# The second network product in float16 pairs, scaled by powers of two

## The chip, the core and the metric

The kernel runs on one core of one Trainium2 chip. The metric is the device time of a launch in microseconds, the median of several runs. The engines are TensorE (PE, its weight loads shown as PEld), VectorE (DVE), ScalarE (ACT), GpSimd (POOL), and SyncE (SP), which issues most DMAs. PSUM holds the products of TensorE until another engine moves them out.

## The reference

An attention block with heads mixed before and after the softmax, then a gated network (SwiGLU) behind an RMS norm. B, H, S, D = 4, 12, 448, 64; DM = 768, DFF = 1536; all inputs float32.

```
scores = q @ k^T / sqrt(D);  scores = einsum('bhij,hg->bgij', scores, w_pre)
attn   = softmax(scores);    attn   = einsum('bhij,hg->bgij', attn, w_post)
x      = (attn @ v) as 1792 tokens x 768
xn     = x / sqrt(mean(x^2) + 1e-6) * rms_g
h      = silu(xn @ w_gate) * (xn @ w_val)        1792 x 1536
out    = h @ w_out                               1792 x 768
```

## The kernel before

Part A (`part_a`, up to about 345 us of the trace) is the attention; it leaves x in DRAM. Part B (`part_b`) is the network, and the change lies there.

A product that must be more exact than one pass of TensorE's narrow types is made of pairs: an operand is split into hi, its value rounded to the narrow type, and lo, the remainder. `product` (L653) does three matmuls for each of six blocks of 128 rows: hi by hi, hi by lo, lo by hi, so 18 matmuls of 128x128 by 128x448 into one PSUM tile. The narrow type is fp32r (float32 storage, "f32" in the rows of matmuls) in some places and float16 in others.

**First product.** The loop over f (12 blocks of 128 columns of the gate and value weights, in the order of `ROWS`, so that blocks of the first and the second half of h take turns) and b (4 batches of 448 tokens) does two `product`s, pg and pv. Rows f = 0 to 3 (f < `PLAIN`) use fp32r pairs, rows 4 to 11 float16 pairs of x (`xn`) and of the weights. The weights come as 64-bit floats; a conversion (`load_w`: `begin`, an Abs on ACT that waits for the DMA of `wraw`, then `half`, four DVE instructions L517 to L520) makes float32 of them. `convert(f)` starts one conversion, if one is due, and gives back its second step. For a float16 row `half` also sums magnitudes (L559), and `even(f + 1, p)` turns the sums into a scale that is a power of two: `largest` (L572 to L578) finds the greatest over all partitions with short DVE instructions, `power` (L585 to L589) makes the power of two and its inverse and copies them to all partitions; then come hi on ACT (L874) and lo on DVE (L875). It was called for p = 0 at b = 2 and p = 1 at b = 3, ahead of `convert`. The outputs' weights (`queue_out`, kind "out") are converted to float32 in rows 5 to 10, at b = 2 and 3, and kept whole in `wos`.

`swiglu` (L683) evicts pg and pv into h: in float16 rows a Silu on ACT and one DVE instruction (L696). h then feeds Strassen's scheme (7 products in place of 8): sums and differences of the blocks of h (first or second half of its 1536 rows, even or odd batch) are made on POOL (L702) and stored to DRAM as `td[0]` to `td[6]`, for two pairs of batches g.

**Second product.** The loop over n (the 7 Strassen products), g (2 pairs of batches) and j (3 blocks of output rows) is 42 units. `hs[n, g]`, one operand, is loaded (`h_load`, `hraw`) and split by `h_split`, two splits per unit: hi on ACT (L643), lo on DVE (L644). The splits run one n ahead of TensorE: twelve are made in f = 11 (b = 2 and 3), so hs[1, 0] is made in the units 0 to 2 of n = 0 and hs[1, 1] in the units 3 to 5. Three buffers (`h_tile`) take turns. The other operand, `fac[n, j]`, is made by `factor`: hi on ACT (L829), lo on POOL (L830); `before` combines weight blocks on POOL (`mix`, L834) ahead of it. A unit's `po` is moved out by ACT for n = 0 (L1025), later by DVE with an addition (L1027).

Every engine works its instructions off in the order of the program, which is written out by hand (`manual_schedule`); a DVE instruction that stands behind a late one is late as well. `ps_p` has 6 PSUM buffers, and one unit of the first product uses two of them.

Of the kernel before, what the change touches and what calls it, by code (L numbers as in the profile page):

```python
# [23 lines left out]
SP_ = 460  # L24
# [24 lines left out]
def attention_moe(ctx: ExitStack, tc, q, k, v, wpre, wpost, mask, ident, wgv, wo, rms_g, out):  # L49
# [473 lines left out]
    def load_w(src, kind, pool_name=None, plain=None):  # L523

        wr, wp_ = b_pools["wr"], b_pools.get(pool_name)
        raws, pair, words = {}, [], {}

        def fetch(p, eng):
            ks = slice(KT * p, KT * p + KT)
            raws[p] = wr.tile([128, KT * 128, 2], I32, name="wraw", tag="wraw", bufs=2)  # L530
            eng.dma_start(raws[p].rearrange("p n t -> p (n t)"), src[:, ks].rearrange("p a f -> p (a f)").bitcast(I32))

        def begin(p):
            raw = raws[p]
            if kind != "out" and not p:
                pair.extend(wp_.tile([128, FT, 128], F32R, name=f"w{n}", tag=f"w{n}") for n in "hl")
            if plain is None:
                c = wr.tile([128, KT * 128], I32, name="wc", tag="wc", bufs=2)
            else:
                c = half.place(2 * half.at + p)  # L540
                plain.append(c)
            words[p] = c
            nc.scalar.activation(c.bitcast(F32), raw.bitcast(F32)[:, :, 1], AF.Abs)

        def half(p):
            raw, c = raws[p], words[p]
            for op in to_f32(raw, c, c)[1:]:
                op()
            if kind == "wide":
                ks = slice(KT * p, KT * p + KT)  # L550
                hi, lo = pair
                f = c.bitcast(F32).rearrange("p (a f) -> p a f", f=128)
                nc.scalar.activation(hi[:, ks], f, AF.Copy)
                nc.gpsimd.tensor_tensor(lo[:, ks], f, hi[:, ks].bitcast(F32), ALU.subtract)
            elif kind == "narrow":
                half.plain.append(c.bitcast(F32))
                if not p:
                    half.sums = b_pools["tiny"].tile([128, 8], F32, name="wsum", tag="wsum", bufs=2)
                nc.scalar.activation(narrow(pair)[0][:, KT * p : KT * p + KT], half.plain[p].rearrange("p (a f) -> p a f", f=128), AF.Abs, scale=2.0 ** -12, accum_out=half.sums[:, p : p + 1])  # L559

        half.fetch, half.begin, half.pair, half.plain = fetch, begin, pair, []
        return half

# [14 lines left out]
        nc.vector.transpose(z[:, 0], z[:, 1])  # L578
        return z[:, 0, :1]

    def power(t, up, more, name):
        o = b_pools["tiny"].tile([128, 3], F32, name=name, tag=name, bufs=2)
# [17 lines left out]
        return t[:, :KT], t[:, KT:]  # L600

    def h_tile(i):
        if i == 0:
            t = b_pools["narrow"].tile([128, 2 * KT, S], F32R, name="hn", tag="xn01")
        else:
            t = b_pools["x3" if i == 1 else "x"].tile([128, 2 * KT, S], F32R, name=f"h{i}", tag="x3" if i == 1 else "x0")
        return t[:, :KT], t[:, KT:]

    raws = {}

# [26 lines left out]
    def h_split(n):  # L637
        for _ in range(min(n, len(hr))):
            i, g, kk, raw = hr.pop(0)
            if kk == 0:  # L640
                hs[i, g] = h_tile((2 * i + g) % 3)
            hi, lo = (t[:, kk] for t in hs[i, g])
            nc.scalar.activation(hi, raw, AF.Copy)  # L643
            nc.vector.tensor_tensor(lo, raw, hi.bitcast(F32), ALU.subtract)  # L644

    def both(ps, w, x, kk):
        (wh, wl), (xh, xl_) = w, x
# [11 lines left out]
            nc.tensor.matmul(ps, a2, xh[:, kk], start=False, stop=(kk == KT - 1))  # L659

    w, xs, wos, fac, hs, hr, keep, unit, xn = {}, {}, {}, {}, {}, [], {}, {}, {}

    conv = {}

# [18 lines left out]
    def swiglu(b, f, pg, pv):  # L683
        half, kk = divmod(ROWS[f], KT)
        i, odd = divmod(b, 2)
        sg = t_tile("sg")
        h = keep["11", i] if not (half or odd) else sg
        if f < PLAIN:
            g, u = (t_tile(n) for n in "gu")
            nc.vector.tensor_tensor(g, pg, ry[b], ALU.mult)  # L690
            nc.scalar.activation(sg, g, AF.Silu)
            nc.vector.tensor_tensor(u, pv, ry[b], ALU.mult)
            nc.gpsimd.tensor_tensor(h, sg, u, ALU.mult)
        else:
            nc.scalar.activation(sg, pg, AF.Silu, scale=unit[f])
            nc.vector.scalar_tensor_tensor(h, pv, unit[f], sg, ALU.mult, ALU.mult)  # L696

        def out_(n, t):
# [93 lines left out]
    def part_b(ps_p):  # L792
# [26 lines left out]
        def factor(n, j):  # L819
            src = block(*((0, 0), (0, 1), (0, 0), (0, 0), (1, 1), (1, 0), (0, 1))[n], j)  # L820
            side = "b" if n % 2 else "a"
            if j == 2 and n % 2 == 0:
                t = b_pools["wr"].tile([128, FT, 128], F32R, name="fac", tag="wraw", bufs=2)
            else:
                pl, tag = (b_pools["keep"], "e1") if j == 2 else (b_pools["w2" + side], ("wh", "wl")[j])
                t = pl.tile([128, FT, 128], F32R, name="fac", tag=tag)
            hi, lo = t[:, :KT], t[:, KT:]
            f = src.rearrange("p (a f) -> p a f", f=128)
            nc.scalar.activation(hi, f, AF.Copy)  # L829
            nc.gpsimd.tensor_tensor(lo, f, hi.bitcast(F32), ALU.subtract)  # L830
            fac[n, j] = hi, lo

        def mix(o, x, y, op=ALU.subtract):
# [29 lines left out]
                nc.vector.tensor_scalar(held["g"], g_sb, up, None, ALU.mult)  # L863
            return held

        def even(f, p, held={}):
            half = halves[f]
            if not p:
                held["up"], unit[f] = power(largest(half.sums, 2), 2, gain(2)["down"], "unit")
                w[f] = narrow(half.pair)  # L870
            up = held["up"]
            hi, lo = (t[:, KT * p : KT * p + KT] for t in w[f])
            c = half.plain[p].rearrange("p (a f) -> p a f", f=128)
            nc.scalar.activation(hi, c, AF.Copy, scale=up)  # L874
            nc.vector.scalar_tensor_tensor(lo, c, up, hi, ALU.mult, ALU.subtract)  # L875

        ahead_x = [(b, kk) for b in range(B) for kk in range(KT)]
        loaded, ry_ps = [], [None]
# [32 lines left out]
        def first_row():  # L911
# [29 lines left out]
            swiglu(2, 0, *first_ps[2])  # L941
            last_rms(0)
            x_fetch(3)

        def last_rms(stage):
            if stage == 0:
# [15 lines left out]
        for f in range(1, FT):  # L962
            plain = f < PLAIN
            for b in range(B):
# [8 lines left out]
                even_next = PLAIN - 1 <= f < FT - 1  # L973
                product(pg, (hi[:, :KT], lo[:, :KT]), x)
                product(pv, (hi[:, KT:], lo[:, KT:]), x)
                if even_next and b >= 2:
                    even(f + 1, b - 2)
                second = convert(f)
                rest = x_narrow(AT_ONCE[f][b]) if plain else None
                second()  # L980
                if plain:
                    rest()
                swiglu(b, f, pg, pv)
                if f == 1 and b == 0:
                    last_rms(1)
# [23 lines left out]
        for n in range(7):  # L1009
            for j, g in units:  # L1010
                po = ps_p.tile([128, S], F32, name="po", tag="p")
                product(po, fac[n, j], hs[n, g])
                h_split(2)
                h_load(4)
                store()
                o = None
# [4 lines left out]
                    stores.append((out[e * 128 : e * 128 + 128, b * S : b * S + S], o))  # L1021
                u_, t_ = u[j, g], t[j, g]
                adds = [[], [(o, u_)], [(u_, u_)], [(t_, u_)], [(o, t_)], [(o, t_), (u_, u_)], [(o, u_)]]
                if not n:
                    nc.scalar.activation(u_, po, AF.Copy)  # L1025
                for dst, add in adds[n]:
                    nc.vector.tensor_tensor(dst, po, add, ALU.add)  # L1027
                if not g:
                    before(n, j)
        store()  # L1030
# [88 lines left out]
```

## Time and profile before

| | us |
|---|---|
| median of 3 runs | 854.97 (850.5 to 855.56) |
| profiled execution | 852.61 |
| its span, first to last instruction | 850.7 |
| PE busy | 815.2 (96%) |
| DVE busy | 613.7 (72%) |
| ACT busy | 420.4 (49%) |
| POOL busy | 360.7 (42%) |

Part A ends and part B begins near 345 us. The fp32r rows of the first product take the time up to 473.9 us, its float16 rows 473.9 to 693.0, the second product 693.0 to 846.9. A row of the timeline gives the start in us, the duration in us, engine, line of the kernel, operation, what it writes and reads, shapes, and in brackets the idle time before it and what ended it. Ends of matmuls are modelled, so the distance between two starts is what is read of them.

### The profile page before, as it was taken

To read this page: it belongs to the slowest core of one execution; us is meant where nothing else is said; L and a number is where in the kernel's file an instruction comes from. 1 tells how busy PE (TensorE), PEld (TensorE's weight loads), DVE (VectorE), ACT (ScalarE), POOL (GpSimd) and SP (SyncE) were. 2 spreads that over 40 slices of the span, in tenths; PEclk is the share of its full clock that TensorE was granted. 3 is DMA by queue.
4 is the path that set the end of the run, shared out by engine and by line. 5 is a ranking of instruction groups with operands and counts; after the bars stand their busy time and mean duration, and the time that the engine had idled before them with its cause. 6 is when DMAs were issued, how large, how long until landed. Compare 5 with 4: busy or idle time off the path is not lost.

```text
span 850.7 us, 26665 instructions
## 1 busy us (share of the span) xinstructions
PE 815.2 (96%) x10900; PEld 608.1 (71%) x10900; DVE 613.7 (72%) x1119; ACT 420.4 (49%) x931; POOL 360.7 (42%) x497
## 2 busy tenths in 40 slices
PE   6899998999999899899999999999999999999998
PEld 2557686777777787689999555555555569999997
DVE  5777686788777676779678867777877459976561
ACT  3677675777767676653334243423333246353310
POOL 8233444555545347944663511212112168572210
PEclk9999998999999999999999999999999999999999
DMA  7687567866855654663655354665647257564641
GB/s 215 200 231 229 165 216 209 238 183 192 246 184 179 197 172 130 187 219 118 196 161 166 108 156 150 198 191 158 194 115 251 76 162 216 161 186 130 173 131 65
DMA packets 81021, 150.07 MB, mean 176 GB/s; under 512 B 10767, under 2 KB 70317, under 8 KB 80899
## 3 DMA queue, kind: packets, MB, share of 16 engines
q1 hardware_dynamic: 76286, 134.72, 52.1%
q0 software_dynamic: 3648, 11.31, 4.9%
q10 hardware_dynamic: 965, 2.34, 0.8%
q8 instruction: 86, 1.41, 0.7%
q14 instruction: 36, 0.29, 0.1%
HBM read 77.55 MB, written 31.21 MB: 128 GB/s over the span
## 4 chain that ended last, share of the span: by engine, by line
PE 75%; DVE 9%; DMA 7%; issue 4%; ACT 2%; POOL 2%; SPq 0%; DVEq 0%; POOLq 0%; ACTq 0%
PE pm L226 9%; PE sp L185 8%; PE qk L137 8%; PE av L270 7%; PE po L659 6%; PE po L657 6%; PE po L658 6%; PE pv L659 4%; PE pv L658 4%; PE pv L657 4%; PE pg L658 4%; PE pg L659 4%; PE pg L657 4%; DMA r<-st 3%; DMA xs<-xd 2%
## 5 line engine op out<-in xcount | busy, mean ns | idle before, releaser
L185 PE MATMUL sp<-r,wk_pre 64*64 64x448 f32 x720 | 165.9, 547 | 5.4 <-DMA r<-st 1.6
L137 PE MATMUL qk<-k,q 64*64 64x448 f32 x768 | 156.8, 564 | 5.9 <-DMA q<-in_q 4.3
L199 ACT ACTIVATE e<-sp,nm 128x448 f32<-128x448 f32 x180 | 114.5, 639 | 90.6 <-DVE nm L192 88.9
L192 DVE TENSOR_REDUCE nm<-sp 128x1 f32<-128x448 f32 x180 | 111.6, 623 | 60.5 <-PE qk L137 32.1
L226 PEld LDWEIGHTS pm<-wn,e 60*64 60x64 f32 x5152 | 110.6, 135 | 48.0 <-POOL wn L211 21.3
L211 POOL TENSOR_SCALAR wn<-wk,rp 128x60 f32<-128x60 f32 x180 | 55.8, 322 | 163.1 <-DVE rp L208 138.7
L226 PE MATMUL pm<-wn,e 60*64 60x60 f32 x5152 | 109.1, 221 | 14.3 <-issue 11.2
L702 POOL TENSOR_TENSOR keep<-sg,keep 128x448 f32<-128x448 f32 x24 | 28.8, 1202 | 164.0 <-DVE sg L696 119.7
L270 PE MATMUL av<-at_all,v 64*64 64x240 f32 (+4 forms) x1728 | 94.9, 321 | 3.3 <-issue 3.3
L185 PEld LDWEIGHTS sp<-r,wk_pre 64*64 64x64 f32 x720 | 62.3, 134 | 24.2 <-issue 10.8
L270 PEld LDWEIGHTS av<-at_all,v 64*64 64x64 f32 x1728 | 71.1, 134 | 6.3 <-issue 5.9
L137 PEld LDWEIGHTS qk<-k,q 64*64 64x64 f32 x768 | 55.1, 136 | 26.5 <-issue 7.3
L659 PE MATMUL pv<-xn,wl 128*128 128x448 f16 x192 | 67.7, 352 | 0.6 <-DVE wl L875 0.6
L657 PE MATMUL pv<-xn,wh 128*128 128x448 f16 x192 | 67.7, 352 | 0.3 <-ACT wh L874 0.3
L657 PE MATMUL pg<-xn,wh 128*128 128x448 f16 x192 | 67.7, 353 | 0.0
L658 PE MATMUL pv<-xn,wh 128*128 128x448 f16 x192 | 67.7, 352 | 0.0
L658 PE MATMUL pg<-xn,wh 128*128 128x448 f16 x192 | 67.7, 352 | 0.0
L659 PE MATMUL pg<-xn,wl 128*128 128x448 f16 x192 | 67.7, 352 | 0.0
L239 DVE COPY at_all<-pm 128x420 f32<-128x420 f32 x92 | 54.3, 591 | 16.8 <-PE pm L226 16.4
L830 POOL TENSOR_TENSOR fac<-wo,fac 128x768 fp32r<-128x768 f32 x21 | 42.2, 2027 | 51.6 <-ACT fac L829 51.6
L659 PEld LDWEIGHTS <-wl 128*128 128x128 f16 x384 | 37.6, 98 | 36.1 <-DVE wl L875 1.1
L657 PEld LDWEIGHTS <-wh 128*128 128x128 f16 x384 | 37.6, 98 | 35.7 <-ACT wh L874 0.7
(169 smaller groups left out, 1883.5 us busy)
## 6 DMA issues: line engine op xcount, KB each, us to landing
r<-st SPq DMA_DIRECT2D x117, 210.0 KB
hraw<-td SPq DMA_DIRECT2D x84, 224.0 KB
wraw<-in_wgv SPq DMA_DIRECT2D x20, 768.0 KB
td<-keep SPq DMA_DIRECT2D x48, 224.0 KB
wraw<-in_wo SPq DMA_DIRECT2D x12, 768.0 KB
r<-st SPq DMA_DIRECT2D x44, 175.0 KB
v<-in_v SPq DMA_DIRECT2D x24, 256.0 KB
q<-in_q POOLq DMA_DIRECT2D x28, 192.0 KB, 5.4
```

The costliest lines, as they stand in the source:

```text
L137: nc.tensor.matmul(ps[j][m, :S], qt[n][sl, hp, m], kt[n // NC, hp][sl], start=True, stop=True)
L185: nc.tensor.matmul(o, wk_pre[sl], rt[n][sl, 2 * p + v_], start=True, stop=True)
L192: nc.vector.tensor_reduce(t, ps[:, :S], AX.X, ALU.max, negate=True)
L199: nc.scalar.activation(e, ps[:, :S], AF.Exp, bias=nmx.pop((n, p, u)), accum_out=sm[n, p][:, u : u + 1])
L211: nc.gpsimd.tensor_scalar(wn[n, p][:, u], wk, r[:, u : u + 1], 1.0, ALU.mult, ALU.mult)
L226: nc.tensor.matmul(o[:, :, at_], e[u_][sl, j : j + JT], w_, start=True, stop=True)
L239: nc.vector.tensor_copy(dst, src)
L270: nc.tensor.matmul(x, vt[b, hp][sl, j, c_], a, start=(c_ == 0), stop=(c_ == JC - 1))
L657: nc.tensor.matmul(ps, a, xh[:, kk], start=(kk == 0), stop=False)
L658: nc.tensor.matmul(ps, a, xl_[:, kk], start=False, stop=False)
L659: nc.tensor.matmul(ps, a2, xh[:, kk], start=False, stop=(kk == KT - 1))
L830: nc.gpsimd.tensor_tensor(lo, f, hi.bitcast(F32), ALU.subtract)
```

## The change

h and the outputs' weights become float16 pairs (hi and lo are both float16) in place of fp32r pairs. Float16 has a narrow range, so both are first multiplied by powers of two, which come from sums of magnitudes; the inverses are multiplied in when `po` is evicted from PSUM.

- `magnitude`: an Abs on ACT with the sum of each partition as a second result, for each of the 12 "out" halves (in `half`) and, through `count`, for each of the 48 tiles of h, one unit after `swiglu` made it.
- `scale_out(j, stage)`: `largest` and `power` for a block j of outputs' weights, and its four pieces multiplied in place on ACT; in rows f = 7 and 9 over b = 0 to 3, and for j = 2 in f = 11 at b = 0 and 1.
- `scale_of(n, cols)`: a DVE reduce (or three) over columns of sums, `largest`, `power`, and one multiplication for the inverses. `scale_of(0)`, for td[0], in f = 11 at b = 0; `scale_of(1)`, for g = 0 of the others, in f = 11 at b = 3, ahead of that unit's `swiglu`; `scale_of(2)`, for g = 1 of the others, in n = 0, unit j = 1 of g = 0, after that unit's two splits.
- `h_split`: hi is a copy with a scale; lo is one DVE instruction that multiplies, then subtracts hi.
- The evictions multiply by the inverse, `down`.
- `even` no longer takes p: at b = 2 it does the scale and both hi parts at once, behind `convert`'s first step, and both lo parts after `convert`'s second step.

```diff
+            else:
+                at_ = 48 + 2 * (half.at % 2) + p
+                magnitude(c.bitcast(F32), KT * 128, small[0][:, at_ : at_ + 1])
...
-            nc.scalar.activation(hi, raw, AF.Copy)
-            nc.vector.tensor_tensor(lo, raw, hi.bitcast(F32), ALU.subtract)
+            sc = scale_h[1 + g if i else 0]
+            nc.scalar.activation(hi, raw, AF.Copy, scale=sc)
+            nc.vector.scalar_tensor_tensor(lo, raw, sc, hi, ALU.mult, ALU.subtract)
...
+    def magnitude(x, n, out_):
+        nc.scalar.activation(small[1].bitcast(F16)[:, :n], x, AF.Abs, scale=2.0 ** -12, accum_out=out_)
+
+    def count():
+        for b, f, h in marks:
+            (g, odd), (half, kk) = divmod(b, 2), divmod(ROWS[f], KT)
+            at_ = ((2 * g + half) * 2 + odd) * KT + kk
+            magnitude(h, S, small[0][:, at_ : at_ + 1])
+        marks.clear()
...
+        def even(f):
...
+            for c, hi, lo in parts:
+                nc.scalar.activation(hi, c, AF.Copy, scale=up)
+
+            def rest():
+                for c, hi, lo in parts:
+                    nc.vector.scalar_tensor_tensor(lo, c, up, hi, ALU.mult, ALU.subtract)
+
+            return rest
+
+        def scale_out(j, stage):
+            if stage == 0:
+                o = small[0][:, 64 + 3 * j : 67 + 3 * j]
+                power(largest(small[0][:, 48:64], 4), 0, None, None, o)
+            for c in wos[2 * j + stage // 2][stage % 2 :][:1]:
+                c = c.bitcast(F32)
+                nc.scalar.activation(c, c, AF.Copy, scale=small[0][:, 65 + 3 * j : 66 + 3 * j])
+
+        def scale_of(n, cols):
+            t = small[0][:, 100 : 104]
+            for i, x in enumerate(cols):
+                nc.vector.tensor_reduce(t[:, i : i + 1], x, AX.X, ALU.max)
+            if len(cols) > 1:
+                nc.vector.tensor_reduce(t[:, :1], t[:, : len(cols)], AX.X, ALU.max)
+            o = small[0][:, 80 + 3 * n : 83 + 3 * n]
+            scale_h[n], down = power(largest(t, 1), 0, None, None, o)
+            downs = small[0][:, 64:73].rearrange("p (j c) -> p j c", c=3)[:, :, 2]
+            nc.vector.tensor_scalar(small[0][:, 90 + 3 * n : 93 + 3 * n], downs, down, None, ALU.mult)
...
-                if even_next and b >= 2:
-                    even(f + 1, b - 2)
-                second = convert(f)
-                rest = x_narrow(AT_ONCE[f][b]) if plain else None
-                second()
+                todo_ = [convert(f)]
+                if even_next and b == 2:
+                    todo_.append(even(f + 1))
                 if plain:
-                    rest()
+                    todo_.append(x_narrow(AT_ONCE[f][b]))
+                count()
+                for x in todo_:
+                    x()
+                if f in (FT // 2 + 1, FT // 2 + 3):
+                    scale_out((f - FT // 2) // 2, b)
+                if f == FT - 1:
+                    if b == 0:
+                        scale_out(2, 0)
+                        scale_of(0, [small[0][:, :KT], small[0][:, 24 : 24 + KT]])
+                    if b == 1:
+                        for i in range(1, 4):
+                            scale_out(2, i)
+                    if b == 3:
+                        scale_of(1, [small[0][:, :24]])
                 swiglu(b, f, pg, pv)
...
                 product(po, fac[n, j], hs[n, g])
+                if n == j == g == 0:
+                    count()
                 h_split(2)
+                if not n and not g and j == 1:
+                    scale_of(2, [small[0][:, 24:48]])
...
-                    nc.scalar.activation(u_, po, AF.Copy)
+                    nc.scalar.activation(u_, po, AF.Copy, scale=down)
                 for dst, add in adds[n]:
-                    nc.vector.tensor_tensor(dst, po, add, ALU.add)
+                    nc.vector.scalar_tensor_tensor(dst, po, down, add, ALU.mult, ALU.add)
```

The tiles of h (`h_tile`) and of the weights (`factor`) keep their sizes in bytes and their places.

## Rows read from the trace of the kernel before

**Rows 1.** Busy us of each engine by stretch: PE, PEld, DVE, ACT, POOL, PEclk, DMA.

```profile
480.00:640.00 160.00, 160.00 (x847) 82.76 (x846) 120.93 (x200) 54.31 (x85) 31.22 (x26) 1.00 0.54 159
692.00:720.00 28.00, 28.00 (x141) 25.63 (x139) 26.02 (x17) 14.59 (x28) 23.68 (x12) 1.00 0.74 230
720.00:760.00 40.00, 40.00 (x198) 36.85 (x198) 32.79 (x35) 17.62 (x31) 25.13 (x12) 1.00 0.59 174
```

**Rows 2.** Tile po: durations in ns (min/median/max), first and last start in us.

```profile
L659 PE MATMUL po<-h,fac x162: 360/363/369, 704.4 to 846.5; 128*128 128x448 f32 x162
...
L657 PE MATMUL po<-hn,fac x90: 360/366/529, 693.0 to 835.2; 128*128 128x448 f32 x90
```

**Rows 3.** Tile xn, the same view.

```profile
L657 PE MATMUL pg<-xn,wh x192: 352/352/363, 473.9 to 689.2; 128*128 128x448 f16 x192
...
L659 PE MATMUL pv<-xn,wl x192: 352/352/363, 479.0 to 693.0; 128*128 128x448 f16 x192
```

**Rows 4.** Timeline of PE, 475.5 to 480.5 us: start, duration, line, operation, idle before.

```profile
477.17 0.35 PE L659 MATMUL pg<-xn,wl 128*128 128x448 f16 x1
477.82 0.36 PE L657 MATMUL pv<-xn,wh 128*128 128x448 f16 x1 [0.30 <-ACT wh L874]
...
479.02 0.36 PE L659 MATMUL pv<-xn,wl 128*128 128x448 f16 x1 [0.65 <-DVE wl L875]
```

**Rows 5.** Timeline of DVE, 466 to 480 us: ends of a chain of twelve.

```profile
467.33 0.17 DVE L572 COPY wsum<-wsum 64x2 f32<-64x2 f32 x1
...
470.18 0.16 DVE L589 COPY unit<-unit 64x2 f32<-64x2 f32 x1
```

**Rows 6.** Timeline of DVE, 570 to 585 us, row f = 7.

```profile
571.77 1.05 DVE L573 COPY wsum<-wsum 32x4 f32<-32x4 f32 x1
...
575.16 0.16 DVE L589 COPY unit<-unit 64x2 f32<-64x2 f32 x1
...
577.32 0.55 DVE L517 TENSOR_SCALAR wo<-wo 128x768 f32<-128x768 f32 x1
...
579.50 0.96 DVE L520 SCALAR_TENSOR_TENSOR wo<-wraw,wo 128x768 int32<-128x768 int32 x1
```

**Rows 7.** Timeline of POOL, the same stretch.

```profile
571.68 1.13 POOL L702 TENSOR_TENSOR keep<-sg,keep 128x448 f32<-128x448 f32 x1 [11.84 <-DVE sg L696]
```

**Rows 8.** Timeline of DVE, 686 to 694 and 709 to 716 us.

```profile
691.20 0.62 DVE L644 TENSOR_TENSOR hn<-hraw,hn 128x448 fp32r<-128x448 f32 x1 [0.93 <-ACT hn L643]
693.43 0.68 DVE L696 SCALAR_TENSOR_TENSOR sg<-pv,unit,sg 128x448 f32<-128x448 f32 x1 [1.60 <-PE pv L659]
...
708.36 6.66 DVE L644 TENSOR_TENSOR h<-hraw,h 128x448 fp32r<-128x448 f32 x3
```

**Rows 9.** Timeline of POOL, 692 to 722 us, and line 830's durations (ns).

```profile
712.29 4.43 POOL L834 TENSOR_TENSOR wo<-wo 128x768 f32<-128x768 f32 x2
716.68 2.24 POOL L830 TENSOR_TENSOR fac<-wo,fac 128x768 fp32r<-128x768 f32 x1
...
L830 POOL TENSOR_TENSOR fac<-wo,fac x21: 1819/1919/2285, 671.0 to 808.7; 128x768 fp32r<-128x768 f32 x21
```

**Rows 10.** Timeline of ACT, 557 to 587 us.

```profile
562.93 0.84 ACT L559 ACTIVATE wh<-wc 128x768 f16<-128x768 f32 x1 [3.69 <-DVE wc L520]
563.68 0.19 ACT L559 ACTIVATION_READ_ACCUMULATOR wh<-wc 128x1 f32 x1
```

**Rows 11.** Lines 627 and 875: durations in ns, min/median/max.

```profile
L627 DVE SCALAR_TENSOR_TENSOR x<-raw,g_sb,x x6: 673/676/1822, 374.4 to 378.5; 128x448 fp32r<-128x448 f32 x6
...
L875 DVE SCALAR_TENSOR_TENSOR wl<-wc,unit,wh x16: 1006/1018/1890, 471.4 to 662.9; 128x768 f16<-128x768 f32 x16
```

**Rows 12.** Timeline of SP's DMA issues and of ACT, 557 to 592 us.

```profile
562.90 0.33 SPq L531 DMA_DIRECT2D wraw<-in_wo  x1
...
580.53 0.33 SPq L531 DMA_DIRECT2D wraw<-in_wgv  x1
...
585.72 0.92 ACT L543 ACTIVATE wc<-wraw 128x768 f32<-128x768 f32 x1 [4.08 <-DMA wraw<-in_wgv]
```

More of the change, by code (lines that the diff above doesn't have):

```diff
@@ L579, in largest, with power @@
         return z[:, 0, :1]
-    def power(t, up, more, name):
-        o = b_pools["tiny"].tile([128, 3], F32, name=name, tag=name, bufs=2)
+    def power(t, up, more, name, o=None):
+        if o is None:
+            o = b_pools["tiny"].tile([128, 3], F32, name=name, tag=name, bufs=2)
         p, s_, inv = (o[:, i : i + 1] for i in range(3))
@@ L602, in h_tile @@
     def h_tile(i):
[L603 to L607, printed above, removed]
+        pl, tag = (("narrow", "xn01"), ("x3", "x3"), ("x", "x0"))[i]
+        t = b_pools[pl].tile([128, 4 * KT, S], F16, name=f"h{i}", tag=tag)
+        return t[:, :KT], t[:, KT : 2 * KT]
     raws = {}
@@ L661, in attention_moe @@
     w, xs, wos, fac, hs, hr, keep, unit, xn = {}, {}, {}, {}, {}, [], {}, {}, {}
+    scale_h, marks, small = {}, [], []
+    def magnitude(x, n, out_):
[6 more added lines that the diff above has]
+        marks.clear()
     conv = {}
@@ L696, in swiglu @@
             nc.vector.scalar_tensor_tensor(h, pv, unit[f], sg, ALU.mult, ALU.mult)
+        marks.append((b, f, h))
         def out_(n, t):
@@ L822, in factor @@
             if j == 2 and n % 2 == 0:
-                t = b_pools["wr"].tile([128, FT, 128], F32R, name="fac", tag="wraw", bufs=2)
+                t = b_pools["wr"].tile([128, 2 * FT, 128], F16, name="fac", tag="wraw", bufs=2)
             else:
                 pl, tag = (b_pools["keep"], "e1") if j == 2 else (b_pools["w2" + side], ("wh", "wl")[j])
-                t = pl.tile([128, FT, 128], F32R, name="fac", tag=tag)
-            hi, lo = t[:, :KT], t[:, KT:]
+                t = pl.tile([128, 2 * FT, 128], F16, name="fac", tag=tag)
+            hi, lo = t[:, :KT], t[:, KT:FT]
             f = src.rearrange("p (a f) -> p a f", f=128)
             nc.scalar.activation(hi, f, AF.Copy)
-            nc.gpsimd.tensor_tensor(lo, f, hi.bitcast(F32), ALU.subtract)
+            nc.gpsimd.tensor_tensor(lo, f, hi, ALU.subtract)
             fac[n, j] = hi, lo
@@ L864, in gain @@
             return held
-        def even(f, p, held={}):
+        def even(f):
             half = halves[f]
[L868 to L875, printed above, removed]
+            up, unit[f] = power(largest(half.sums, 2), 2, gain(2)["down"], "unit")
+            w[f] = narrow(half.pair)
+            parts = [(c.rearrange("p (a f) -> p a f", f=128), *(t[:, KT * p : KT * p + KT] for t in w[f])) for p, c in enumerate(half.plain)]
+            for c, hi, lo in parts:
[21 more added lines that the diff above has]
+            nc.vector.tensor_scalar(small[0][:, 90 + 3 * n : 93 + 3 * n], downs, down, None, ALU.mult)
         ahead_x = [(b, kk) for b in range(B) for kk in range(KT)]
@@ L943, in first_row @@
             x_fetch(3)
+            small.extend(const.tile([128, SP_], F32, name=n, tag="sum", bufs=2) for n in ("small", "junk"))
         def last_rms(stage):
@@ L1023, in part_b @@
                 adds = [[], [(o, u_)], [(u_, u_)], [(t_, u_)], [(o, t_)], [(o, t_), (u_, u_)], [(o, u_)]]
+                k_ = 90 + 3 * (1 + g if n else 0) + j
+                down = small[0][:, k_ : k_ + 1]
                 if not n:
-                    nc.scalar.activation(u_, po, AF.Copy)
+                    nc.scalar.activation(u_, po, AF.Copy, scale=down)
                 for dst, add in adds[n]:
-                    nc.vector.tensor_tensor(dst, po, add, ALU.add)
+                    nc.vector.scalar_tensor_tensor(dst, po, down, add, ALU.mult, ALU.add)
                 if not g:
```

## The prediction

> **What bounds the kernel now.** The busy times by stretch come first [rows 1]. In the stretches that the change touches TensorE is busy from end to end, at the full granted clock (1.00, the 2.4 GHz level): the reader is to see 28.00 of 28 us and 40.00 of 40. So what counts is the step from one matmul's start to the next one's, and the places where TensorE stood waiting. The second network product (tile po: 42 units, each 18 matmuls and an eviction, 756 matmuls in all) starts at 693.0 and its last matmul at 846.5 [rows 2]: 153.5 / 755 = 203.3 ns a step. The gate and value products of float16 pairs (tile xn, 1152 matmuls of the same 128x128 by 128x448) start at 473.9, the last one at 693.0 [rows 3]: 219.1 us over 1151 steps. Three of these, from 477.17 to 479.02, hold two waits [rows 4]: 1.85 us where three steps are 0.57, so 1.28 too long; (219.1 - 1.28) / 1151 = 189.2 ns. The type makes 14.1 ns a matmul. The profiled run took 852.61 us, of which the span is 850.7.
>
> Next, the vector engine (DVE) and GpSimd (POOL) at the start of the second product: busy 26.02 and 23.68 of 28 us [rows 1]. A split on DVE (L644, two inputs in SBUF) takes 0.62 alone, at 691.20, but three take 6.66 at 708.36 [rows 8], 2.2 each, as long as the POOL instructions beside them [rows 9]: DVE gets one such instruction done for each of POOL's, until POOL pauses at 716.68 + 2.24 = 718.9. The short instructions that find a scale show the same in an earlier row of units: L573, a copy of four numbers, took 1.05 and ended at 571.77 + 1.05 = 572.82 [rows 6], POOL's L702 at 571.68 + 1.13 = 572.81 [rows 7].
>
> **The matmuls, a gain of 10.6 us.** h and the outputs' weights become float16 pairs of the shapes of [rows 3], so the step is taken as 189.2: 755 x 14.1 ns = 10.6. Bounds: nothing (third rival), and 10.7, by the rows' rounding.
>
> **The weights of the next row, a gain of 1.3 us.** even() now does both parts at b = 2; before, the second came at b = 3, and the two waits of [rows 4] were for its wh and wl. At b = 2 of that row the chain L572 to L589 ends at 470.34 [rows 5]. Two copies on ACT and two subtractions of 1.0 us alone [rows 11], 1.9 beside POOL, follow with some 1.3 us of other work: done by 475.5, ahead of the 477.82 at which they are wanted. So 1.3, with 0 as the other end.
>
> In rows f = 5 to 10 these subtractions now stand behind the four conversion instructions, and the copies behind the Abs that waits for wraw. Take f = 7. The chain ends at 575.3 [rows 6], conversion (L517 to L520) takes 580.46 - 577.32 = 3.1, two subtractions 2.0: 580.4. Row f = 8 starts at 473.9 + 1.3 + 4 x 144 x 0.1892 = 584.2. The wraw in question was issued at 562.90; one issued at 580.53 let its reader start at 585.72 [rows 12], 5.2 later, so it lands near 568, before ACT gets to the Abs. Cost nothing; the cover is 3.8 us a row, and past it each us is paid once a row.
>
> **Magnitudes and scalings on ACT, cost nothing.** 48 Abs over h and 12 over weights, each with a read of its sum, cost at most the 0.84 + 0.19 of the 768-column one [rows 10]; with 12 scalings of 768 columns at about 1 us, 74 us of ACT in the 455 from the first. ACT was busy 14.59 of 28 us at most [rows 1]; an h is read a unit after it is made, and nothing on TensorE waits for a magnitude alone. Evictions become three-operand instructions, 0.68 as the swiglu's at 693.43 where a two-operand one takes 0.62 [rows 8]; six PSUM buffers cover them, but for the last: 0.06 us.
>
> **The third scale, a cost of 4.7 us.** scale_of is a reduce, the twelve instructions L572 to L589 and a multiplication, about 3.4 us (3.0 by [rows 5], and 0.4). scale_out and scale_of(0) fall where DVE may trail by a unit. scale_of(1), at f = 11 and b = 3, stands behind the split that ends at 691.82 and ahead of the swiglu at 693.43 [rows 8]: that swiglu starts near 695.2, and POOL's burst, which begins with its result, shifts by 1.8. scale_of(2), in unit j = 1 of n = 0, stands between splits 4 and 5 of hs[1, 0]. Split 4 ended at 708.36 + 2.2 = 710.6, now at 712.4. POOL instructions, which ended at 712.3, 714.5, 716.7 and 718.9 [rows 9], now do so at 714.1, 716.3, 718.5 and 720.7. Four of the chain's instructions move two or more numbers of a row (L573, L577, L588, L589); by [rows 6, 7] each waits for one of these ends. So the scale is there at 720.7, and splits 5 and 6 at 721.6 and 722.3. TensorE wants split 5's low half as matmul 121 after the first: 693.0 + 121 x 0.1892 = 715.9 (before, 717.6). It waits 5.7. With less of DVE against it POOL is faster (L830: 1.82 to 2.29 [rows 9]), which may give 1 back: 4.7. The ends: if the chain runs free, it is through at 715.8, and split 5 waits for the POOL end at 716.3 or 718.5, split 6 for the next, so about 2; if POOL gains nothing, 6. I take 4.7, since the row nearest to it (L573) shows the lock in full. Behind it, hs[1, 1] is wanted from 728 on, and POOL pauses, because its next factors wait for ACT's copies, which stand behind the same scale. Later on POOL is busy 25.13 of 40 us, against 23.68 of 28 [rows 1].
>
> **Sum.** -10.6 - 1.3 + 4.7 + 0.1 = -7.1: 852.61 becomes 845.5. The profiled run lies 2.4 under the median of the three (854.97); the mean of all four is 853.4, which becomes 846.3. I say 846.
>
> A rule of the Trainium skill speaks against the new split, which multiplies and subtracts in one three-operand instruction: "Vector Engine (DVE) Microarchitecture Reference", section 7, "Points that are easy to get wrong", says that this form, with two SBUF inputs that aren't bf16, runs at half the throughput. The rows disagree with it (fourth rival). By the page the sum would be about 2 us worse.
>
> **Rivals.** First, no wait at the third scale: POOL's burst thins out, or the chain is through before it matters. For it: each L830 stands behind a copy on ACT, which leaves holes. Against it: [rows 8, 9]. A gain of 11.8, so 841.5. Chance 0.17.
>
> Second, more waits than that one. hs[0, 1] keeps about 1 us of cover after the shift by 1.8, and in rows f = 1 to 3 DVE runs behind TensorE (the wait of [rows 4] is its doing) and now has magnitudes between its conversions, on ACT. Two or three waits of 1 to 3 us leave a gain of 0 to 4: 849 to 853. Chance 0.18.
>
> Third, the step isn't the type's, and the change doesn't do what it says. For it: the two products ran beside different traffic, a DMA share of 0.54 against 0.74 and 0.59 [rows 1]. Against it: the float16 steps stayed at 189 whatever ran beside them. Then -1.3 + 4.7 + 0.1 leaves 856 to 857. Chance 0.04.
>
> Fourth, splits at half rate. The three-operand form took 1.02 us for 768 columns and 0.68 for 448 [rows 11], 1.06 ns a column, so one a cycle of DVE's; doubled, a split takes 1.15. Splits 5 and 6 of hs[1, 0] come 0.9 later and the next six use up their cover: 848. Chance 0.03.
>
> Fifth, on the other side, slower: in rows f = 4 to 10 the subtractions behind the conversion come late for the next row. Slower by over 1% needs 8.5 + 7.1 = 15.6 us lost, over seven rows 2.2 each, so a lateness of 3.8 + 2.2 = 6.0 in every row, for instance by wraw landing at 577 or the new Abs holding up ACT's copies: from 862 on. Against it: DVE is busy 120.93 of 160 us there [rows 1], 20.6 of the 27.2 of a row, and only rows 7 and 9 get a chain more. Chance 0.06.
>
> **How the numbers follow.** My forecast, a wait of 2 to 6 us at the third scale alone, has 0.52: 843.5 to 848, likeliest 846. Over 1%, 8.5 us, is about what a measurement of this kernel can tell from no change. A third of the forecast's cases (0.17), with a wait under 3.3 us, and the first rival (0.17) pass it: faster 0.34. Slower 0.06; the rest, 0.60, is within 1%. The range from 840.5 to 852.5 takes in the first rival and most of the second, with the scatter of 2.5 us that the runs show; it leaves out the slower cases and about one in ten below it and above.
>
> **What would show it.** Right: a step of po of 189 ns; no wait ahead of row f = 4; one wait of 3 to 6 us in the seventh unit of po, put down to DVE's h, and in the chain ahead of it L573, L577, L588 and L589 at 1 to 2 us each. Wrong: that chain free of POOL, waits in units 3 to 5 of po or late ones, or waits for wl at the start of rows 5 to 11.

## The result, and the profile after

The change brought no gain. The comparison gave 854.54 us against 848.86 for the kernel before, medians of 20 runs each, and a ratio of 1.0051 (95% interval 1.0031 to 1.0072). This ratio and those below are worked out from the fast runs (one of the changed kernel, 861.93 us, was slow), so they are not quite the quotients of the medians. On two more chips the ratio was 0.9997 (0.9967 to 1.0027) and 0.9992 (0.9962 to 1.0022), and the kernel before against itself gave 0.9965 (0.9935 to 0.9996), so a few tenths of a per cent are not to be read from one comparison. What is to be explained is that a gain of about 12 us, all of it there, was given back: 846 was forecast, and 850.9 to 854.5 came.

The profiled execution of the changed kernel took 851.36 us, its span 849.4. The attention, which the change leaves alone, differs by 3.2 us between the two profiled executions, so part B is compared by itself, from the first matmul of the first product to the last matmul: 346.0 to 846.5 before, 342.8 to 845.2 after, 500.5 and 502.4 us. Later executions gave 501.4 for the kernel before, 501.7 and 501.1 for the changed one. All these lengths are differences of starts read to 0.1 us.

From the page of the changed kernel: busy time of PE, the chain that ended last by engine, and two groups of matmuls (busy us and mean ns, idle time before them and its releaser).

```profile
PE 804.5 (95%) x10900; PEld 538.4 (63%) x10900; DVE 633.1 (75%) x1199; ACT 477.2 (56%) x1063; POOL 355.6 (42%) x497
...
PE 47%; DVE 27%; issue 8%; ACT 8%; DMA 7%; POOL 2%; SPq 1%; ACTq 0%; DVEq 0%; POOLq 0%
...
L662 PE MATMUL po<-h,fac 128*128 128x448 f16 x252 | 89.9, 357 | 6.2 <-DVE h L648 6.2
...
L663 PE MATMUL pg<-xn,wl 128*128 128x448 f16 x192 | 67.7, 353 | 4.3 <-DVE wl L893 4.3
```

Most of the loss is in the two idle times: TensorE waits 6.2 us for low halves of h, and 4.3 us for low halves of gate and value weights. Its busy time by stretch (columns as in [rows 1]) shows where:

```profile
480.00:640.00 160.00, 157.63 (x833) 81.23 (x832) 122.42 (x215) 79.23 (x152) 29.68 (x24) 1.00 0.53 155
692.00:720.00 28.00, 24.74 (x130) 12.57 (x129) 26.29 (x42) 14.23 (x25) 21.16 (x12) 1.00 0.68 214
...
720.00:760.00 40.00, 37.10 (x184) 18.65 (x184) 33.04 (x38) 20.80 (x34) 23.55 (x14) 0.91 0.63 191
```

In [rows 1] PE was busy for the whole of all three. The timeline of PE has four long waits (start, duration, idle before the matmul in brackets):

```profile
637.25 0.36 PE L663 MATMUL pg<-xn,wl 128*128 128x448 f16 x1 [2.16 <-DVE wl L893]
...
666.60 0.36 PE L663 MATMUL pg<-xn,wl 128*128 128x448 f16 x1 [1.93 <-DVE wl L893]
...
708.35 0.35 PE L662 MATMUL po<-h,fac 128*128 128x448 f16 x1 [1.42 <-DVE h L648]
...
722.90 0.53 PE L662 MATMUL po<-h,fac 128*128 128x448 f16 x1 [4.75 <-DVE h L648]
```

Counted as the step from one matmul's start to the next, less the 0.19 of a free one, that is 2.3 us at the start of row f = 10, 2.1 at f = 11 (and 0.4 at f = 9), 1.6 in the fourth unit of the second product ("unit 3"), and 4.9 in the seventh ("unit 6"). During the last one the granted clock fell to 0.50, the 1.2 GHz level, and stayed there for 4.8 us behind it:

```profile
721.00:727.50 6.50, 4.60 (x13) 1.92 (x13) 6.07 (x10) 5.47 (x10) 0.98 (x1) 0.50 0.54 160
```

Thirteen matmuls came 0.37 us apart there in place of 0.19, 2.3 us more. The losses in order: 4.8 + 1.6 + 4.9 + 2.3 = 13.6 us. On the other side stand the 10.6 and 1.3 us of the prediction's first two terms. -11.9 + 13.6 = +1.7, against a measured 502.4 - 500.5 = +1.9.

### The profile page after: what moved, and what is told of

It is laid out like the page before. It is cut to its first block, busy times and chain, and to the rows that moved or that the text cites. A ratio compares the mean times of both kernels' runs of the same rounds, so it can differ in the third digit from the quotient of the medians.

```text
span 849.4 us, 26853 instructions
## 1 busy us (share of the span) xinstructions
PE 804.5 (95%) x10900; PEld 538.4 (63%) x10900; DVE 633.1 (75%) x1199; ACT 477.2 (56%) x1063; POOL 355.6 (42%) x497
## 4 chain that ended last, share of the span: by engine, by line
PE 47%; DVE 27%; issue 8%; ACT 8%; DMA 7%; POOL 2%; SPq 1%; ACTq 0%; DVEq 0%; POOLq 0%
PE pm L226 9%; PE qk L137 8%; PE sp L185 8%; PE av L270 7%; PE po L662 5%; PE po L663 5%; PE po L661 5%; DVE wc L519 3%; DVE wc L518 3%; DMA xs<-xd 2%; DMA r<-st 2%; DVE wc L520 2%; DVE wc L517 2%; ACT wc L543 2%; DVE wo L519 1%
## 5 line engine op out<-in xcount | busy, mean ns | idle before, releaser
L185 PE MATMUL sp<-r,wk_pre 64*64 64x448 f32 x720 | 163.7, 539 | 4.2 <-DMA r<-st 2.5
L137 PE MATMUL qk<-k,q 64*64 64x448 f32 x768 | 152.3, 554 | 6.0 <-DMA q<-in_q 4.1
L662 PE MATMUL po<-h,fac 128*128 128x448 f16 x252 | 89.9, 357 | 6.2 <-DVE h L648 6.2
L661 PE MATMUL po<-h,fac 128*128 128x448 f16 x252 | 89.7, 356 | 0.0
L663 PE MATMUL po<-h,fac 128*128 128x448 f16 x252 | 89.7, 356 | 0.0
L648 DVE SCALAR_TENSOR_TENSOR h<-hraw,small,h 128x448 f16<-128x448 f32 x84 | 82.7, 1027 | 7.8 <-ACT h L647 7.7
L647 ACT ACTIVATE h<-hraw,small 128x448 f16<-128x448 f32 x84 | 51.6, 659 | 49.3 <-PE po L663 28.6
L661 PE MATMUL pg<-xn,wh 128*128 128x448 f16 x192 | 67.7, 352 | 0.0
```

Of the source, the lines that this page charges most:

```text
L137: nc.tensor.matmul(ps[j][m, :S], qt[n][sl, hp, m], kt[n // NC, hp][sl], start=True, stop=True)
L185: nc.tensor.matmul(o, wk_pre[sl], rt[n][sl, 2 * p + v_], start=True, stop=True)
L647: nc.scalar.activation(hi, raw, AF.Copy, scale=sc)
L648: nc.vector.scalar_tensor_tensor(lo, raw, sc, hi, ALU.mult, ALU.subtract)
L661: nc.tensor.matmul(ps, a, xh[:, kk], start=(kk == 0), stop=False)
L662: nc.tensor.matmul(ps, a, xl_[:, kk], start=False, stop=False)
```

## The loop that falls behind

The waits at rows 9 to 11 were not in the sum, so their cause was looked for first. DVE's swiglu instruction of a row's last block (b = 3), in rows f = 6 to 10 of the changed kernel:

```profile
554.89 0.68 DVE L711 SCALAR_TENSOR_TENSOR sg<-pv,unit,sg 128x448 f32<-128x448 f32 x1 [1.58 <-ACT sg L710]
...
586.11 0.68 DVE L711 SCALAR_TENSOR_TENSOR sg<-pv,unit,sg 128x448 f32<-128x448 f32 x1 [2.41 <-ACT sg L710]
...
613.81 0.68 DVE L711 SCALAR_TENSOR_TENSOR sg<-pv,unit,sg 128x448 f32<-128x448 f32 x1 [1.58 <-ACT sg L710]
...
645.02 0.68 DVE L711 SCALAR_TENSOR_TENSOR sg<-pv,unit,sg 128x448 f32<-128x448 f32 x1 [2.41 <-ACT sg L710]
...
672.72 0.69 DVE L711 SCALAR_TENSOR_TENSOR sg<-pv,unit,sg 128x448 f32<-128x448 f32 x1 [1.58 <-ACT sg L710]
```

Rows 7 to 10 take 31.2, 27.7, 31.2 and 27.7 us, where TensorE needs 144 x 0.1892 = 27.2. In each of these five lines, DVE's idle time ends with ACT's Silu, not with TensorE's product: DVE and ACT pace each other. The end of row 8 shows how. ACT, then DVE, same stretch:

```profile
612.32 0.84 ACT L669 ACTIVATE junk<-wo 128x768 f16<-128x768 f32 x1 [2.47 <-DVE wo L520]
613.07 0.19 ACT L669 ACTIVATION_READ_ACCUMULATOR junk<-wo 128x1 f32 x1
613.16 0.61 ACT L710 ACTIVATE sg<-pg,unit 128x448 f32<-128x448 f32 x1
613.68 0.89 ACT L543 ACTIVATE wc<-wraw 128x768 f32<-128x768 f32 x1
```

```profile
611.27 0.96 DVE L520 SCALAR_TENSOR_TENSOR wo<-wraw,wo 128x768 int32<-128x768 int32 x1
613.81 0.68 DVE L711 SCALAR_TENSOR_TENSOR sg<-pv,unit,sg 128x448 f32<-128x448 f32 x1 [1.58 <-ACT sg L710]
614.61 0.56 DVE L517 TENSOR_SCALAR wc<-wc 128x768 f32<-128x768 f32 x1
```

The magnitude of the outputs' weights (junk<-wo) cannot begin before DVE has made the last quarter of the conversion (L520, done at 612.23). The Silu stands behind it on ACT, the swiglu (L711) waits for the Silu, and the next conversion (L517) stands behind the swiglu, and its Abs on ACT (L543) behind the Silu. DVE idles 1.58 us, though TensorE was through with row 8 at 606.9. In rows 7 and 9 `scale_out` adds a chain on DVE and a scaling on ACT, again ahead of the Silu. So a row with conversions has no time to spare, and whatever a row is late stays for the next one. The subtractions that make wl for the next row drift with the loop (DVE, in rows 6 and 8, both subtractions in one line):

```profile
547.70 1.94 DVE L893 SCALAR_TENSOR_TENSOR wl<-wc,unit,wh 128x768 f16<-128x768 f32 x2
...
606.61 1.94 DVE L893 SCALAR_TENSOR_TENSOR wl<-wc,unit,wh 128x768 f16<-128x768 f32 x2
```

They lie 58.9 us apart, 29.5 a row against TensorE's 27.2. The first of the two was done 4.1 us before row 7's third matmul wanted it, 1.8 us before row 8's, and after that each row's third matmul waited: 0.4, 2.3 and 2.1 us.

## The experiments

Two theories stood at the start, for two different losses. The loop just shown, for rows 9 to 11; and, for units 3 and 6, the chains of `scale_of` in DVE's queue, stretched by POOL. The rival was that the losses come from something the scales only accompany (the float16 pairs themselves, the new order of `even`, other traffic). The first four kernels ran on one chip, where the kernel before took 853.7 us (845.83 to 859.04).

**Magnitudes and scaling out of the loop.** The weights' magnitudes wait for the next `count()`, which takes h's; `scale_out` goes behind `swiglu`.

```diff
-                magnitude(c.bitcast(F32), KT * 128, small[0][:, at_ : at_ + 1])
+                out_marks.append((c.bitcast(F32), at_))
...
         marks.clear()
+        for c, at_ in out_marks:
+            magnitude(c, KT * 128, small[0][:, at_ : at_ + 1])
+        out_marks.clear()
...
-                if f in (FT // 2 + 1, FT // 2 + 3):
-                    scale_out((f - FT // 2) // 2, b)
                 swiglu(b, f, pg, pv)
+                if f in (FT // 2 + 1, FT // 2 + 3):
+                    scale_out((f - FT // 2) // 2, b)
```

> The changed kernel with one order altered: the magnitudes of the outputs' weights wait for the next unit's count, and scale_out stands behind swiglu, so ACT reaches Silu without first waiting for DVE's conversion. Theory 'loop' (in rows 7 to 10 DVE waits for Silu, Silu stands on ACT behind magnitudes and scalings that wait for DVE; a row with scale_out takes about 31 us against TensorE's 27.2): the waits at the starts of rows 9, 10 and 11 (0.4, 2.3 and 2.1 us) are gone, 4.8 us less than the changed kernel, and the waits in the second product stay at about 9 us. Rival 'order of even' (the subtractions come late because they stand behind the conversion): all three waits stay and the time is that of the changed kernel.

Measured: 844.18 us, ratio 0.9907 (0.9875 to 0.9938). No wait at rows 9 to 11, none at unit 3, and 3.7 us with a shorter stretch at half clock at unit 6. Part B took 494.0, 8.4 less than the changed kernel's first trace where 4.8 was expected. The waits in the second product were expected to stay and did not: the lag of the rows had pushed the splits of h back.

**The scales of h one place on.** `scale_of(1)` a block earlier, `scale_of(2)` a unit later, where fewer things wait behind them.

```diff
-                    if b == 3:
+                    if b == 2:
                         scale_of(1, [small[0][:, :24]])
...
-                if not n and not g and j == 1:
+                if not n and not g and j == 2:
                     scale_of(2, [small[0][:, 24:48]])
```

> The changed kernel with scale_of(1) at b = 2 of row 11 in place of b = 3, and scale_of(2) one unit later, behind splits 5 and 6 of hs[1, 0]. Theory 'third scale': the wait of 4.9 us in unit 6 of the second product, the half clock behind it (2.5 us more) and most of the 1.6 us in unit 3 are gone, 7.4 to 9 less than the changed kernel; rows 9 to 11 keep their 4.8. Rival 'moved only': the chain beside POOL's burst makes hs[1, 1] late instead, a wait of 3 us or more appears in units 9 to 11, and the time falls by under 4.

Measured: 845.89 us, ratio 0.9919 (0.9889 to 0.9949), part B 495.0. The wait at unit 6 and the half clock are gone, 4.2 us stay at rows 10 and 11, and about 2 us are lost in small waits of units 0 to 8. Part B is 7.4 us below the changed kernel's first trace, the low end of the 7.4 to 9 expected.

**Both.**

> Both alterations of order. If the two causes are separate and the only ones: no wait over 0.3 us from row 4 on, part B 13 to 14 us shorter than in the changed kernel, and a ratio to the kernel before of 0.986 to 0.990. If something else costs time as well (other parts of the program, the clock), the ratio stays above 0.992 though the waits are gone.

Measured: 839.94 us, ratio 0.988 (0.9845 to 0.9914), below both kernels and the best version found. Part B took 488.6 us: 11.9 less than before, the sum of the first two terms, with every scale in place. Taken singly the two alterations gave 8.4 and 7.4 us, more than the 13.8 of both, so the causes are not quite separate: the rows' lag also lengthens the waits of units 3 and 6. Its busy times by stretch, and DVE's third scale:

```profile
692.00:720.00 28.00, 28.00 (x150) 14.48 (x148) 24.21 (x30) 14.95 (x27) 21.64 (x12) 1.00 0.69 217
720.00:760.00 40.00, 40.00 (x214) 20.69 (x212) 33.64 (x37) 22.80 (x39) 24.08 (x13) 1.00 0.62 182
```

```profile
710.59 0.17 DVE L911 TENSOR_REDUCE small<-small 128x1 f32<-128x24 f32 x1
...
716.07 0.23 DVE L917 TENSOR_SCALAR small<-small 128x3 f32<-128x3 f32 x1
```

TensorE is busy throughout, although the chain still takes 716.30 - 710.59 = 5.7 us beside POOL: it is not shorter by much, but nothing that TensorE needs soon stands behind it.

**No scales.** All magnitudes, `scale_out` and `scale_of` left out; the scales are 1, the instructions that use them stay.

> The float16 pairs alone: no magnitudes, no scale_out, no scale_of; every scale is read from memory as before but holds 1. The computation of the scales is left out. All that the type, the new splits and even's new order give: 10.7 (matmuls) + 1.3 (row 4) = 12 us under the kernel before, a ratio of 0.986, with no waits in rows 5 to 11. If the new order of even is itself late, waits at the starts of rows 9 to 11 are still there, 2 to 5 us in all.

Measured: 840.14 us, ratio 0.9865 (0.9833 to 0.9897), part B 488.7. The float16 pairs, the three-operand splits and evictions and the new `even` cost nothing by themselves; all of the loss belongs to making the scales. Tile po there, the same view as [rows 2]:

```profile
L661 PE MATMUL po<-h,fac x252: 352/352/353, 690.3 to 832.8; 128*128 128x448 f16 x126
...
L663 PE MATMUL po<-h,fac x252: 352/352/353, 690.7 to 833.2; 128*128 128x448 f16 x126
```

(833.2 - 690.3) / 755 = 189.3 ns a step, 203.3 before.

The next four ran on another chip, where the kernel before took 852.65 us (845.83 to 860.4).

**The changed kernel again.**

> The changed kernel once more, beside the others of this group, for a second trace and a ratio from the same chip. Theory (the loop of VectorE and ScalarE in rows 7 to 10, and the third scale): again 1.003 to 1.009 of the kernel before; waits of 4.8 us in all at rows 9 to 11, about 1.6 us at unit 3 and 5 us at unit 6 of the second product, and a stretch at half clock behind unit 6. Rival (what made it slow is not in the first product's last rows or the scales, but outside, in the part that did not change): the waits come out at other places or sizes, and the ratio moves with them.

Measured: 850.9 us, ratio 0.9997, below the expected 1.003 to 1.009. The waits came at the same places: 4.1 us in rows 10 and 11, 1.6 at unit 3, 4.9 at unit 6, then 6.8 us at half clock; part B 501.7. So part B's losses are the kernel's own, and the rest of the first ratio's 0.5% is not found in it.

**POOL without the combinations.** `mix` left out for n = 0 (`if n == 0` became `if n == 99`), so POOL is free for much of the burst.

> Leaves out GpSimd's combinations of the output weights ahead of the second product's first step (the splits of the weights stay on GpSimd). Theory (GpSimd's instructions stretch VectorE's small copies and its subtractions): the chain of the third scale takes about 3.3 us where it took 7.1, the subtractions ahead of it 0.68 us each where they took 1.5 to 2.2, so the waits at units 3 and 6 (1.6 and 4.9 us) and the half clock behind them go; the waits at rows 9 to 11 stay at 4 to 5 us; about 9 us less than the changed kernel, 0.994 to 0.996 of the kernel before. Rival (the chain is late by its own dozen instructions and its place in the queue, whatever GpSimd does): 2 to 4 us of the wait at unit 6 stay, and it gains 2 to 4 us.

Measured: 844.99 us, ratio 0.991 (0.9878 to 0.9943); part B 493.4, 8.3 less than the changed kernel on this chip where about 9 was expected; waits at units 3 and 6 gone, those of rows 10 and 11 (4.1 us) unmoved. The chain of the third scale, from the timelines of DVE and POOL, first in the changed kernel:

```profile
715.55 1.22 DVE L577 COPY small<-small 32x2 f32<-32x2 f32 x1
716.80 0.14 DVE L578 TENSOR_REDUCE square<-small 32x1 f32<-32x4 f32 x1
...
717.42 1.12 DVE L581 TENSOR_SCALAR square<-small 1x32 f32<-1x32 f32 x1
...
719.22 1.19 DVE L593 COPY small<-small 32x2 f32<-32x2 f32 x1
720.44 1.56 DVE L594 COPY small<-small 64x2 f32<-64x2 f32 x1
722.03 0.23 DVE L914 TENSOR_SCALAR small<-small 128x3 f32<-128x3 f32 x1
```

```profile
714.72 2.02 POOL L847 TENSOR_TENSOR fac<-wo,fac 128x768 f16<-128x768 f32 x1
716.71 3.67 POOL L851 TENSOR_TENSOR wo<-wo 128x768 f32<-128x768 f32 x2
720.34 1.63 POOL L847 TENSOR_TENSOR fac<-wo,fac 128x768 f16<-128x768 f32 x1
```

and then without the combinations:

```profile
717.04 1.22 DVE L577 COPY small<-small 32x2 f32<-32x2 f32 x1
...
718.91 0.17 DVE L581 TENSOR_SCALAR square<-small 1x32 f32<-1x32 f32 x1
...
719.76 0.16 DVE L593 COPY small<-small 32x2 f32<-32x2 f32 x1
719.95 0.16 DVE L594 COPY small<-small 64x2 f32<-64x2 f32 x1
```

In the changed kernel L577 ends at 716.77, L593 at 720.41 and L594 at 722.00, each within 0.05 of an end of POOL's (716.74, 720.38, 721.97); L581 ends at 718.54, when the first of the two L851 makes way for the second. Left alone, L581, L593 and L594 take 0.17, 0.16 and 0.16 where they took 1.12, 1.19 and 1.56, and the chain 3.7 us (716.66 to 720.38) in place of 7.1; only L577 still meets a POOL instruction (716.39 to 718.24). The Trainium skill has the rule, in "SBUF — State Buffer", "Who interferes with whom": a port pair shared by DVE and GpSimd is held for a whole instruction, which copies and tensor_scalar can ask for, and a reduce never does. The rows agree: L578, a reduce, took 0.14 beside the same POOL work.

**One half of the loop's load at a time.** First only the magnitudes moved (the first two hunks of the first experiment), then only `scale_out` (the last).

> The changed kernel with only the output weights' magnitudes moved, from ahead of the Silu that comes next to the following place where h's magnitudes are taken; the scaling of the output weights stays ahead of the Silu. Theory (the loop's lag piles up over rows, because rows 8 and 10 with the magnitudes take 27.7 us where TensorE takes 27.2 and so never catch up; without them they take 26.0): rows 7 and 9 take 29 to 30 us, rows 8 and 10 about 26, the lag never passes the cover of 3.8 us, and of the 5.2 us of waits at rows 9 to 11 at most 0.7 us is left; units 3 and 6 wait as before or up to 1.5 us less. 0.996 to 1.002 of the kernel before. Rival (the scaling, its chain and its copy ahead of each Silu in rows 7 and 9, is what is too long): 3 us or more of the row waits stay, 1.001 to 1.006.

> The changed kernel with only the scaling of the output weights moved, from ahead of rows 7 and 9's swiglu to behind it; the magnitudes stay ahead of the Silu. Theory (the magnitudes keep rows 8 and 10 from catching up): rows 7 and 9 take 30 to 31 us, rows 8 and 10 still 27.7, and 2.5 to 5 us of the 5.2 us of row waits stay; 1.000 to 1.007 of the kernel before. Rival (the scaling ahead of the Silu is the cause): rows 7 and 9 fall to 28 us or less and the row waits are gone, 0.996 to 1.000.

Measured: magnitudes alone 843.47 us, ratio 0.9903 (0.987 to 0.9936), no wait at rows 9 to 11, part B 491.5. Scaling alone 853.17 us, ratio 1.0008 (0.9976 to 1.004), 3.1 us still lost at row 10, part B 502.0. Length of a row by the last L711 (or its counterpart) of each, in us:

| row f | 7 | 8 | 9 | 10 |
|---|---|---|---|---|
| changed kernel | 31.2 | 27.7 | 31.2 | 27.7 |
| magnitudes moved | 27.8 | 26.7 | 27.8 | 26.7 |
| scaling moved | 31.3 | 27.7 | 31.3 | 27.7 |
| both moved | 29.3 | 26.0 | 28.6 | 26.0 |
| no scales | 27.2 | 27.2 | 27.2 | 27.2 |

With the magnitudes out of its way, the Silu is done before it is wanted, and TensorE's product is what DVE waits for (DVE, end of row 8 again):

```profile
606.73 0.96 DVE L520 SCALAR_TENSOR_TENSOR wo<-wraw,wo 128x768 int32<-128x768 int32 x1
608.34 0.68 DVE L714 SCALAR_TENSOR_TENSOR sg<-pv,unit,sg 128x448 f32<-128x448 f32 x1 [0.66 <-PE pv L663]
```

Rows 8 and 10 then catch up, and so do not add to the lag. The theory's sizes were too small here: rows 7 and 9 were expected at 29 to 30 us and took 27.8, unit 3 did not wait at all, unit 6 only 2.9 us, and the half clock stayed away, so the ratio came out lower than expected. The scaling by itself costs little, once the magnitude ahead of it is gone.

The last three ran on a third chip, with the kernel before at 853.44 us (848.15 to 859.99).

**The kernel before against itself, `even` alone, and the changed kernel a third time.** `even` alone is the kernel before with the change's `even` and its place in the loop:

```diff
-                if even_next and b >= 2:
-                    even(f + 1, b - 2)
-                second = convert(f)
...
+                todo_ = [convert(f)]
+                if even_next and b == 2:
+                    todo_.append(even(f + 1))
```

> The kernel before against itself, to see how far two groups of runs of one kernel lie apart and whether its second part takes the same time again. Theory (the two kernels differ by the waits of the second part alone, and the 5.7 us between the first medians held some of the chip's own spread): ratio 0.997 to 1.003, and from the first product's first matmul to the last matmul 500 to 501 us again. Rival (the kernel before has itself a faster and a slower way through its second part): another length there, by 3 us or more.

> The kernel before with one edit of the change alone: both parts of the next row's weights at the third block in place of one each at the third and fourth. Theory: the wait of 1.3 us at the start of row 4 goes and nothing else moves, so the second part takes 1.3 us less, 0.996 to 1.001 of the kernel before. Rival (the subtractions behind the conversion come late in the rows with a conversion in each block, also without magnitudes and scalings): waits of 0.5 us or more at the starts of rows 9 to 11.

> The changed kernel on the chip that this group gets, beside the kernel before against itself. Theory (gains of 12 us and waits with their half clock of 14 to 15 us nearly cancel): 0.999 to 1.007 of the kernel before, and 501.5 to 502.5 us from the first product's first matmul to the last matmul. Rival (the first comparison's 1.005 came from its chip alone): 0.997 to 1.000.

Measured: before against itself 0.9965 (0.9935 to 0.9996), part B 501.4, both just outside what was expected; the rows' wait at f = 4 was 2.2 us there, 1.3 in [rows 4]. `even` alone 849.09 us, 0.997 (0.9936 to 1.0004): not to be told from the kernel before by its time, but part B took 499.3, the wait at f = 4 was gone and no new one came. The changed kernel 851.68 us, 0.9992, part B 501.1 (501.5 to 502.5 was expected), with 2.5 us of waits at rows 10 and 11 (and a stretch at half clock behind the first), 1.6 at unit 3 and 4.9 at unit 6.

## Why the prediction was wrong

**The matmuls, -10.6: right.** 189.3 ns a step without waits; the third rival (the step isn't the type's) is out.

**The weights of the next row, -1.3: right.** The wait is gone in every kernel with the new `even`.

**The third scale, 4.7: right in mechanism, and in size partly by luck.** The wait was 4.9 us, and four small instructions of the chain, the counterparts of the four named, took 1.1 to 1.6 each. But the rows' lag, which the forecast did not have, is in the 4.9: the chain began at 715.16, not 712.4, and TensorE wanted split 5 at 718.0, not 715.9. Without that lag the wait was 3.7 us (magnitudes and scaling moved) and 2.9 (magnitudes alone), which is what 4.7 should be set beside; both lie in the 2 to 6 that the prediction gave. Not in the sum was what follows such a wait: the stretch at half clock, 2.3 us.

**Three-operand splits and evictions: right.** The shortest splits took 0.67 us for 448 columns and the median was 0.68, no slower a column than [rows 11], so the fourth rival is out, and with it, for these shapes, the statement on half the throughput of the Trainium skill's "Vector Engine (DVE) Microarchitecture Reference", section 7.

**"Cost nothing; the cover is 3.8 us a row": this step failed.** It has two halves. `even`'s new place by itself does cost nothing, as the kernel with `even` alone and the one without scales show. But the cover was taken as if each row had it anew. It is a stock that only a row with time to spare refills. Rows 7 to 10 came out 4.0 + 0.5 + 4.0 + 0.5 = 9.0 us over TensorE's time; the cover of the first subtraction at the start of row 7 was 4.1, and the other 4.9 came out as waits, 4.8 measured. The size was about right: by the prediction's count, from the second subtraction's end to the row's start, rows 6 to 11 had 3.9 to 4.5 us in the kernel with `even` alone. The "a row" was wrong. That DVE was busy only 120.93 of 160 us, the argument held against the fifth rival, said nothing either: in the changed kernel it is 122.42, and the loop is full, because DVE's gaps are waits for ACT.

**"Magnitudes and scalings on ACT, cost nothing": failed with it.** ACT had the time, and nothing on TensorE waits for a magnitude, as was said. What was overlooked is what stands behind the magnitude in ACT's own queue: the Silu that DVE waits for. Moving the weights' 12 magnitudes a few places on made part B 10.2 us shorter than the changed kernel's on the same chip (491.5 against 501.7): 4.1 at the rows, 1.6 at unit 3, 2.0 at unit 6 and 2.5 of half clock.

**`scale_of(1)`: underestimated.** The swiglu of that block was forecast near 695.2 and came at 698.31, since the six splits ahead of it were late with the rows, and two POOL instructions ran beside some of them; the cover of about 1 us on hs[0, 1] was gone, and unit 3 waited 1.6. The second rival had this wait, and its 849 to 853 held what the second and third chip gave, but it looked for the others in rows f = 1 to 3, not 9 to 11. The fifth named the right place and the right queue, at a price for which every row would have had to be late by 6.

**The level.** 846 was counted from runs about 853.4; the first comparison had the kernel before at 848.9. So 854.54 lies above the range by 2 us, while within 1%, the case with the largest chance, is what came. The forecast was of a difference, -7.1 us, and by part B it came out at +1.9 in the first pair of traces. Of these 9.0 us, 4.8 + 1.6 + 2.3 are terms left out, and 0.2 lies on the third scale.

## What to carry over

Ask of every instruction added to an engine with time to spare what stands behind it in that engine's queue and who waits for that; a busy share of 50% does not answer it. Where two engines feed each other, add up their round trip over a whole row and compare it with the bottleneck's time for that row: a round trip a little too long costs nothing for some rows, and then all of it. And a chain of tiny instructions belongs where nothing urgent stands behind it: moving two such chains one place on took 7.4 us off part B and kept all the work, where freeing POOL, which shortened the chain to 3.7 us, took 8.3 off and left work out.

## What was not expected of the hardware

A wait of TensorE costs more than its length, but not always. With a wait of 4.9 us the clock was at 0.50 for some 6.8 us in two executions of the changed kernel, the end of the wait included, and for 3.4 in a third; with 4.7 us, the scaling moved, for 6.8; with 3.7 us, in the first experiment, for 3.4; with 2.9 us, the magnitudes moved, not at all. Yet at row 10 it fell for 3.4 us after 3.1 us (scaling moved) and after 2.1 us (third execution), and after the 2.3 of the first it did not. Busy times around two of these waits, with the granted clock as the number after POOL's: the first experiment, then the one with the magnitudes moved.

```profile
718.20:721.60 3.40, 3.40 (x11) 1.36 (x9) 3.22 (x7) 3.40 (x7) 0.00 (x0) 0.50 0.85 246
```

```profile
716.00:728.00 12.00, 12.00 (x65) 6.18 (x64) 11.24 (x15) 11.04 (x19) 5.76 (x4) 1.00 0.68 208
```

What decides it these runs do not show. It makes the end of such a wait uncertain by up to 2.5 us.
